# Windowed attention and token mixing on one core: the first batch in a written order, scores and masks by quarters of the array

## Chip, core and metric

One core of one Trainium2 chip runs the whole kernel. The time is the device time of one execution in microseconds, the median of several runs. The engines are TensorE (PE, with its weight loads shown apart as PEld), VectorE (DVE), ScalarE (ACT), GpSimd (POOL) and SyncE (SP); SP and POOL issue the DMAs of this kernel.

## What is computed

Attention with a window of 128 positions and 4 sink positions, over 4 batches, 8 heads, 768 positions, 64 values a head; then an MLP mixer: a token part that works across the 768 positions and a channel part that works across the 512 channels.

```python
scores = scale * np.matmul(q, k.transpose(0, 1, 3, 2))
is_sink = pos[None, :] < int(n_sink)
in_window = (rel >= 0) & (rel < int(window))
scores = np.where(is_sink | in_window, scores, -1000000000.0)
a = np.exp(scores - np.max(scores, axis=-1, keepdims=True))
a = a / (np.sum(a, axis=-1, keepdims=True) + 1e-09)
x = np.matmul(a, v)                       # heads side by side: (4, 768, 512)
xt = x.transpose(0, 2, 1)
h = np.maximum(xt @ w_tok1, 0.0) @ w_tok2
u = x + h.transpose(0, 2, 1)
h2 = np.maximum(u @ w_ch1, 0.0) @ w_ch2
out = u + h2
```

All inputs and the output are fp32; matmuls run in bf16.

## The kernel before

**Tiling.** Two heads make a pair; there are 16 pairs, four in each batch, numbered p = 0 to 15. Rows of a tile of q or k are 128 groups of 6 positions. A pair's q and k are transposed on PE (line 442 for the first pairs, 460 later), by halves of the rows (64 rows, all 128 columns), into PSUM, and evicted to qT and kT (line 118 on DVE, 116 on ACT), the two heads on partitions 0 to 63 and 64 to 127. Scores are made with keys on partitions: for each tile of 128 keys the 256 queries that its window can reach (lines 496 to 503), three pieces g = 0, 1, 2 of two key tiles each. One exp on ACT (line 509) goes over a piece. The values then follow by `pv` (line 555, first batch) or `sink_values` and `values` (lines 597 and 631), with a column of ones that gives the sum of the weights; DVE takes its reciprocal and multiplies into x_sb (lines 576 and 579, 616 and 619).

**Masks.** In the first batch, for all pieces but one, PE writes the mask into PSUM ahead of the scores: a matmul of the identity with a tile of zeros and -32768 (`masked`, lines 471 to 484, over all 128 rows and columns), to which the scores are added. In the later batches, and for that one piece, DVE multiplies by a mask of zeros and ones after the exp (line 516).

**Sinks.** The first four keys of each pair are copied out of the transposed k into a small tile of their own, `kTs` (`sink_columns`, line 410, two copies a pair). `score_sinks` (line 530) makes the scores of two pairs with them, in four matmuls of 64 rows, 32 columns and 512 queries. The sinks' values of the first batch are loaded by SP in four small DMAs in fp32 (line 188) and cast by POOL (line 984).

**Loads.** q and k of the first four pairs come by SP in fp32, 384 KB each (line 81), and are cast by ACT, DVE or POOL (line 979). SP's program has pairs 0 and 1 first, then the four small loads of the sinks' values, then pairs 2 and 3 (lines 131, 188 and 193). All other q, k, v and the weights come on POOL's queue, cast to bf16 on the way (lines 94, 102, 127); v of pair 0 is issued early, at line 194. The order on that queue is v 0 to 3 with the two token weights among them, pair 4, half of the first channel weight (`w_ch1`, in four quarters), pair 5, and so on.

**Order.** A planner (`Plan`, line 238) runs when the program is built. Each unit of PE work has a cost, what it depends on and the PSUM banks that it needs; other work (casts, evictions, exps, loads) has a cost for each engine that could do it. `run` (line 310) goes through planned time and takes the unit that can begin soonest. In the first batch it chooses among six lists (line 808): scores, masks, transposes, values, and token work of the two halves of the channels. After that the units of channel mixing of one batch (`main`) are mixed with attention and token work of the next (`side`). Nothing is decided on the chip: the engines run their lists in order and wait on semaphores. There are two score banks `sc` (each of 2 x 2 KB a partition) and four banks `mx`.

At the start PE runs seven matmuls on a tile of ones (`keep_warm`, line 138) while the first loads are on their way.

Of the kernel before, what the change touches and what calls it, by code (L numbers as in the profile page):

```python
# [9 lines left out]
FP32 = mybir.dt.float32  # L10
# [6 lines left out]
def kernel(  # L17
# [29 lines left out]
    MASKED_BY_PE = [(p, g) for p in range(NHP) for g in range(NT // 2) if (p, g) != (NHP - 1, 0)]  # L47
# [5 lines left out]
    pt_pool = ctx.enter_context(tc.tile_pool(name="pt", bufs=2))  # L53
# [8 lines left out]

    def bank(tag, *shape, dtype=FP32, slot=None):

        n = given[tag].pop(0) if slot is None else slot
        return psum.tile([P, *shape], dtype, name=f"ps_{tag}", tag=f"{tag}{n}", bufs=1)
# [64 lines left out]
    raws = {p: load_raw(p) for p in range(2)}  # L131
    vs = {}


    ones = singles.tile([P, 4 * P], BF16)
    in_order(nc.vector.memset(ones, 1.0))

    def keep_warm(n, slot):
        ps = bank("mx", 4 * P, slot=slot)
        for _ in range(n):  # L140
            mm(ps, ones[:, 0:P], ones, start=True, stop=True)

    keep_warm(7, 0)


# [4 lines left out]
    MASKED = -32768.0  # L150
    mask_add = singles.tile([P, 4, 2, P], BF16)
    mask_adds = [mask_add[:, ts(n, 2)] for n in range(2)]
    in_order(nc.vector.memset(mask_add, 0.0))
# [12 lines left out]
    ))  # L166
    in_order(nc.gpsimd.memset(mask_add[0:n_sink, 2], 0.0))
# [3 lines left out]
    NKB = 2  # L171
    kTb = [singles.tile([P, S], BF16, name=f"kT{n}") for n in range(NKB)]

    kTs0 = singles.tile([P, NHP, 2, D], BF16, name="kTs")
    kTs = [kTs0[:, n] for n in range(NHP)]
# [6 lines left out]
    in_order(nc.vector.memset(kTs0, 0.0))  # L182
    v_sink_f = singles.tile([P, NHP, 2, D1], FP32)
    in_order(nc.vector.memset(v_sink_f, 0.0))
    for n in range(4):
        i, odd = n // 2, n % 2
        rows = slice(D * i + ODD * odd, D * i + ODD * odd + n_sink)
        in_order(nc.sync.dma_start(
            out=v_sink_f[rows, odd::2, i, 0:D],
            in_=v[0].rearrange("(p o i) s d -> i o s p d", i=2, o=2)[i, odd, 0:n_sink],  # L190
        ))
        in_order(nc.vector.memset(v_sink_f[rows, odd::2, i, D:D1], 1.0))
    raws.update({p: load_raw(p) for p in range(2, NHP)})
    vs[0] = load_v(0)
# [19 lines left out]
    SWITCH = 95.0  # L214
    FIRST = 1800.0
# [22 lines left out]
    class Plan:  # L238
# [59 lines left out]

        def commit_pe(self, op, t):
            for tag, banks in op.need.items():  # L300
                given[tag] = [n for _, n in self.slots(tag)[:len(banks)]]
                for n, readers in zip(given[tag], banks):
                    self.held[tag][n] = readers
            op.fn()
            self.free["PE"] = t + op.cost["PE"] + SWITCH * (op.half != self.half)
            self.half = op.half
            op.done = self.free["PE"] + PE_OUT + SEM
            self.pending.extend(op.then)
# [85 lines left out]
    def prepare(p):  # L394

        kT, ks = kTb[p % NKB], kTs[p % NHP]
# [13 lines left out]
        def sink_columns(e):  # L410
            c = ODD * (p % 2)
            first = (tiles["ps_k", p][:, 0] if parts == 1 else tiles["ps_k", p][0])[:, 0, 0:n_sink]
            for i in range(2):
                copy(e, ks[ds(D * i, D), i, c:c + n_sink], first[ds(D * i, D)])

        free = ([("sk", p - 2)] if p >= 2 else [], [("s", p - NKB)] if p >= NKB else [])
# [4 lines left out]
        for n, name in enumerate(("qT", "kT")):  # L421
# [3 lines left out]
            for part, op in enumerate(done[name, p]):  # L425
                op.urgent = (3 - part) * (p < NHP)
        tiles["kT", p] = kT
        done["kTs", p] = Op(
            {"ACT": 440.0, "DVE": 400.0}, sink_columns, [("sk", p - NHP)] if p >= NHP else [],
        )  # L430

    def turn(p, n):
# [3 lines left out]
        def run():  # L436
            ps = [bank("mx", NT, D, dtype=BF16) for _ in range(2)]
            tiles["ps_" + name, p] = [t.rearrange("d j p -> d p j") for t in ps]
            for j in range(NT):
                for x in range(2):  # L440
                    rows = ds(D * x, D)
                    in_order(nc.tensor.transpose(ps[x][:, j], bfs[p, n][rows, j], ident[rows, rows]))  # L442

        readers = [[op] for op in done[name + "T", p]]
        if n:
            readers[0].append(done["kTs", p])
# [5 lines left out]
    def transposed(p):  # L452

        def run():
            ps = bank("sc", 2, 8 * P, dtype=BF16)[:, :, 0:2 * NT * D].rearrange("d x (n j p) -> d x n j p", n=2, j=NT)
            for n in range(2):
                for j in range(NT):
                    for x in range(2):
                        rows = ds(D * x, D)
                        in_order(nc.tensor.transpose(ps[:, x, n, j], bfs[p, n][rows, j], ident[rows, rows]))  # L460
                tiles["ps_" + "qk"[n], p] = ps[:, :, n].rearrange("d x j p -> d x p j")

        then = [*done["qT", p], *done["kT", p], done["kTs", p]]
# [3 lines left out]

    def width(g):
        return 3 * P if g == NT // 2 - 1 else 4 * P

    def masked(p, g):

        def run():
            ps = tiles["ps_s", p, g] = bank("sc", 2, 4 * P)
            for i in range(2):
                mm(
                    ps[:, i, 0:width(g)], ident,
                    mask_adds[g == 0].rearrange("p k n q -> p (k n q)")[:, 0:width(g)], start=True, stop=False,
                )

        x = done["exp", p, g] = Op({}, None)
        deps = [done["tk", 0]] if p == 0 else []
        done["mask", p, g] = unit(width(g) * 0.84, run, deps, {"sc": [[x]]})
        return done["mask", p, g]

    def scores(p, g):


        by_pe = ("mask", p, g) in done

        def run():
            if ("pT", p) not in tiles:
                tiles["pT", p] = pt_pool.tile([P, 2, NT, 2, P], BF16, name="pT")
            if not by_pe:
                tiles["ps_s", p, g] = bank("sc", 2, 4 * P)
            for k in range(2):
                kt = 2 * g + k
                nq = 2 if kt < NT - 1 else 1
                for i in range(2):
                    mm(  # L500
                        tiles["ps_s", p, g][:, i, ds(2 * k * P, nq * P)], tiles["kT", p][ds(D * i, D), ts(kt, P)],
                        tiles["qT", p][ds(D * i, D), kt * P:(kt + nq) * P], start=not by_pe, stop=True,
                    )
# [4 lines left out]
        def exp(e):  # L508
            in_order(nc.scalar.activation(  # L509
                part(tiles["pT", p][:, :, ds(2 * g, 2)]), tiles["ps_s", p, g][:, :, 0:width(g)], AF.Exp, scale=scale,  # L510
# [7 lines left out]
        x = done["exp", p, g] if by_pe else Op({}, None)  # L518
        x.cost, x.fn, x.deps = {"ACT": 190.0 + 1.5 * width(g)}, exp, [done["pv", p - 2]] if p >= 2 else []
        x.urgent = 2 * (p < NHP)  # L520
        then = [x]
        if not by_pe:
            then.append(Op({"DVE": 100.0 + 1.2 * width(g)}, mask, [x, done["masks"]]))
# [3 lines left out]
        deps += [done["mask", p, g]] if by_pe else []  # L527
        return piece(width(g) * 0.47, run, deps, {} if by_pe else {"sc": [[x]]}, then, [("s", p)])

    def score_sinks(p):  # L530


        def run():
            pT_sink = pt_pool.tile([P, (NT - 2) * P], BF16, name="pT_sink")
            tiles["ps_sk", p] = bank("mx", (NT - 2) * P)
            for n in (p - 1, p):
                tiles["pT_sink", n] = pT_sink
                for i in range(2):
# [3 lines left out]
                        tiles["ps_sk", p][ds(D * i + c, ODD)], kTs[n % NHP][rows, i, ds(c, ODD)],  # L542
# [6 lines left out]
        x = Op({"ACT": 580.0}, exp, [done["pv", p - 2]] if p >= 2 else [])  # L549
        for n in (p - 1, p):  # L550
            done["p", n, NT] = x
        deps = [d for m in (p - 1, p) for d in [done["kTs", m], *done["qT", m]]]
        return piece(225, run, deps, {"mx": [[x]]}, [x], [("sk", p - 1), ("sk", p)])

    def pv(p, half):
# [31 lines left out]
        n.urgent = r.urgent = (1 + 1.5 * (p >= NHP // 2)) * (p < NHP)  # L587
# [9 lines left out]
    def sink_values(p):  # L597
# [4 lines left out]
        def run():  # L602
            for i in range(2):
                tiles["ps_o", p, i] = bank("mx", NT, D1)
            for qt in range(2, NT):
                for i in range(2):
                    rows = ds(D * i, D)
                    mm(
                        tiles["ps_o", p, i][:, qt], tiles["pT_sink", p][rows, ts(qt - 2, P)], vsk[rows, i],
                        start=(qt == 2), stop=False,  # L610
                    )
# [120 lines left out]
    def turned_u(b, g, tag="mx"):  # L732
# [4 lines left out]
        def run():  # L737
            if tag == "sc":
                both = bank("sc", 2, 8 * P, dtype=BF16)[:, :, 0:nct * NT * D]
# [334 lines left out]
```

## Time and profile before

| | |
|---|---|
| median of 3 runs | 209.35 us (209.11 to 209.48) |
| the profiled execution: its time | 209.19 us |
| its span in the profile | 207.4 us |
| instructions | 5087 |
| HBM read / written | 26.75 MB / 6.29 MB |
| POOL's DMA queue (q0) | 67232 packets, 11.80 MB |
| SP's DMA queue (q1) | 5968 packets, 9.45 MB |
| exps of the window's scores on ACT (line 509) | 48, 44.3 us |
| first channel matmul (`uT,w_ch`) | starts at 31.2 us |
| first matmul of the second channel weight (`w_ch,v1T`) | starts at 53.0 us |

Busy times of the engines overlap, so they don't add up to the span. Line 109 is the helper through which all matmuls are recorded; they are told apart by the names of the tiles written and read. `64*128` is a matmul that uses 64 rows and 128 columns of the array. Matmuls are pipelined: the duration of one has the way through the array in it, so what a matmul costs in a row of them is read from the distance of the starts. Times in lines of the timeline and of windows are from the start of the span.

### The profile page before, as it was taken

The numbers are of one execution on the slowest core, as the hardware profiler recorded it, in microseconds if no ns is written. First come the engines' busy times: TensorE is split into PE (matmuls) and PEld (weight loads), VectorE is DVE, ScalarE is ACT, GpSimd is POOL, SyncE is SP. The second block draws the span as 40 slices with busy tenths as digits, with TensorE's granted clock in tenths as the row PEclk, the third lists the DMA queues.
The fourth block names the chain that finished last, engine by engine and source line by source line (L and its number), as shares of the span: only waits on it lengthen the run. The fifth ranks groups of instructions, "written<-read, shape, count | busy, mean of one in ns | idle before, by whom it ended". The sixth has DMA issues, their size and how long they took to land.

```text
span 207.4 us, 5087 instructions
## 1 busy us (share of the span) xinstructions
PE 200.7 (97%) x2161; PEld 119.5 (58%) x2161; DVE 114.7 (55%) x246; ACT 113.9 (55%) x208; POOL 67.2 (32%) x86
## 2 busy tenths in 40 slices
PE   6899999999999999999999999999999999999994
PEld 2355885566665565557656645666756445665443
DVE  4686654757768666866586462767583521000222
ACT  4699767868807526868584141869651103773000
POOL 6199678696499991630000000000000000000000
PEclk9999999999999999999999999999999999999999
DMA  6999999999999999695001112100001122000222
GB/s 204 281 240 148 167 187 183 165 166 199 167 174 156 215 174 204 71 82 38 3 0 55 51 54 101 51 5 0 3 0 54 51 101 104 0 0 0 101 104 101
DMA packets 73223, 21.57 MB, mean 104 GB/s; under 512 B 63217, under 2 KB 70257, under 8 KB 73201
## 3 DMA queue, kind: packets, MB, share of 16 engines
q0 software_dynamic: 67232, 11.80, 72.3%
q1 hardware_dynamic: 5968, 9.45, 12.9%
q8 instruction: 17, 0.28, 0.5%
q14 instruction: 6, 0.04, 0.1%
HBM read 26.75 MB, written 6.29 MB: 159 GB/s over the span
## 4 chain that ended last, share of the span: by engine, by line
PE 91%; DVE 4%; DMA 2%; ACT 2%; issue 0%; SPq 0%
PE ps_mx L109 77%; PE ps_sc L109 8%; PE ps_sc L460 2%; DMA k_f<-in_k_dram 2%; PE ps_mx L442 1%; DVE x_sb L619 1%; DVE kT L118 1%; PE ps_mx L749 1%; ACT qT L116 1%; PE ps_mx L112 1%; ACT pT L509 0%; DVE uT L118 0%; ACT v1T L122 0%; DVE recip L616 0%; DVE u_sb L720 0%
## 5 line engine op out<-in xcount | busy, mean ns | idle before, releaser
L109 PE MATMUL ps_mx<-uT,w_ch 128*128 128x384 bf16 x384 | 68.3, 326 | 1.3 <-DVE x_sb L619 0.9
L109 PE MATMUL ps_mx<-w_ch,v1T 128*128 128x512 bf16 (+2 forms) x312 | 65.7, 363 | 0.0
L122 ACT ACTIVATE v1T<-ps_mx 128x384 bf16<-128x384 f32 x74 | 36.2, 492 | 28.7 <-PE ps_mx L109 18.3
L509 ACT ACTIVATE pT<-ps_sc 128x1024 bf16<-128x1024 f32 (+1 forms) x48 | 44.3, 952 | 11.3 <-PE ps_sc L109 10.8
L109 PEld LDWEIGHTS <-w_ch 128*128 128x128 bf16 x384 | 35.3, 98 | 26.1 <-DVE x_sb L619 3.1
L109 PEld LDWEIGHTS <-v1T 128*128 128x128 bf16 x312 | 29.0, 98 | 29.0 <-issue 0.2
L888 DVE TENSOR_TENSOR o_sb<-ps_mx,u_sb 128x512 f32<-128x512 f32 x23 | 15.9, 690 | 39.3 <-PE ps_mx L109 39.0
L94 POOL DMA_DIRECT2D q_bf<-in_q_dram x24 | 19.7, 823 | 5.6 <-DMA w_ch<-in_moe_w_ch_dram 2.2
L109 PEld LDWEIGHTS <-w_tok 128*128 128x128 bf16 x192 | 18.4, 98 | 4.6 <-issue 0.7
L94 POOL DMA_DIRECT2D k_bf<-in_k_dram x24 | 19.6, 820 | 3.7 <-DMA w_ch<-in_moe_w_ch_dram 3.7
L118 DVE COPY kT<-ps_sc 128x768 bf16<-128x768 bf16 x11 | 10.5, 958 | 17.3 <-ACT qT L116 17.3
L102 POOL DMA_DIRECT2D v_aug<-in_v_dram x16 | 16.4, 1028 | 9.4 <-ACT pT L509 6.2
L720 DVE TENSOR_TENSOR u_sb<-ps_mx,x_sb 128x512 bf16<-128x512 f32 x20 | 12.7, 685 | 8.3 <-PE ps_mx L109 8.3
L516 DVE TENSOR_TENSOR pT<-pT,mask_main 128x1024 bf16<-128x1024 bf16 (+1 forms) x24 | 14.5, 619 | 2.5 <-ACT pT L509 2.5
L109 PE MATMUL ps_sc<-qT,kT 64*128 64x256 bf16 x192 | 15.9, 270 | 0.0
L109 PE MATMUL ps_mx<-v_aug,pT 128*128 128x65 bf16 x352 | 15.3, 194 | 0.0
L109 PEld LDWEIGHTS <-pT 128*128 128x128 bf16 x352 | 13.6, 98 | 2.3 <-issue 0.6
L124 DVE TENSOR_SCALAR v1T<-ps_mx 128x384 bf16<-128x384 f32 x22 | 12.1, 554 | 3.8 <-PE ps_mx L109 3.3
L116 ACT ACTIVATE qT<-ps_sc 128x768 bf16<-128x768 bf16 x11 | 8.9, 811 | 7.5 <-PE ps_sc L460 7.3
L109 PE MATMUL ps_mx<-h1T,w_tok 128*128 128x256 bf16 x96 | 12.6, 273 | 0.0
L109 PE MATMUL ps_mx<-x_sb,w_tok 128*128 128x256 bf16 x96 | 12.0, 273 | 0.0
L619 DVE TENSOR_TENSOR x_sb<-ps_mx,recip 128x384 bf16<-128x384 f32 x22 | 11.4, 551 | 0.1
(72 smaller groups left out, 153.7 us busy)
## 6 DMA issues: line engine op xcount, KB each, us to landing
out_dram<-o_sb SPq DMA_DIRECT2D x23, 256.0 KB, 2.0
v_aug<-in_v_dram POOLq DMA_DIRECT2D x16, 192.0 KB, 6.5
w_ch<-in_moe_w_ch_dram POOLq DMA_DIRECT2D x8, 384.0 KB, 8.7
q_bf<-in_q_dram POOLq DMA_DIRECT2D x24, 96.0 KB, 6.7
k_bf<-in_k_dram POOLq DMA_DIRECT2D x24, 96.0 KB, 5.6
q_f<-in_q_dram SPq DMA_DIRECT2D x4, 384.0 KB, 5.9
k_f<-in_k_dram SPq DMA_DIRECT2D x4, 384.0 KB, 6.2
w_tok<-in_moe_w_tok_dram POOLq DMA_DIRECT2D x2, 384.0 KB, 7.4
```

Of the source, the lines that this page charges most:

```text
L94: in_order(nc.gpsimd.dma_start(out=out[:, h], in_=rows[:, h]))
L102: in_order(nc.gpsimd.dma_start(out=v_aug.rearrange("p i t d -> p (i t) d")[:, :, 0:D], in_=v[b].rearrange("h s d -> (h s) d")[2 * hp * S:2 ...
L109: in_order(nc.tensor.matmul(*args, skip_group_check=True, **kwargs))
L116: in_order(nc.scalar.activation(out, in_, AF.Copy))
L118: in_order({"DVE": nc.vector, "POOL": nc.gpsimd}[e].tensor_copy(out=out, in_=in_))
L122: in_order(nc.scalar.activation(out, in_, AF.Relu))
L124: in_order(nc.vector.tensor_scalar_max(out=out, in0=in_, scalar1=0.0))
L509: in_order(nc.scalar.activation(part(tiles["pT", p][:, :, ds(2 * g, 2)]), tiles["ps_s", p, g][:, :, 0:width(g)], AF.Exp, scale=scale,))
L516: in_order(nc.vector.tensor_tensor(out=pt, in0=pt, in1=m, op=ALU.mult))
L619: in_order(nc.vector.tensor_tensor(out=x_sb[b][:, :, ds((2 * hp + i) * D, D)], in0=tiles["ps_o", p, i][:, :, 0:D], in1=tiles["recip", p, i ...
L720: in_order(nc.vector.tensor_tensor(out=u_part(b, g, s0, n), in0=tiles["ps_u", b, g, s0], in1=x_sb[b][:, s0:s0 + n, c0:c0 + cn], op=ALU.add,))
L888: in_order(nc.vector.tensor_tensor(out=o_sb.rearrange("p (g c) -> p g c", g=2), in1=u_rows(b, st), in0=tiles["ps_out", b, st].rearrange("p ...
```

## The change

Seven edits go together.

- **SP's queue** has the eight loads of q and k of the first four pairs back to back. The sinks' values are loaded by POOL in four DMAs straight into the bf16 tile; the fp32 tile and its cast go. v of pairs 0 and 1 are issued by the planner, after the casts of q of pairs 1 and 2, instead of at the head of the program.
- **Quarters.** Transposes, scores and the sinks' values use 64 rows and 64 columns of the array, where they used 64 rows and 128 columns: a transpose or a score matmul becomes two. A quarter of 64 keys is scored against 192 queries (256 for the first), the blocks of the score bank that no quarter writes are filled once by ACT with -32768. Where a transposed tile overwrites such a block, DVE clears it (`cleared`).
- **Masks of the first batch** are added inside the unit of the scores, by quarters (`add_masks`): four matmuls of 64x64 by 256 columns and two by 64. This now holds for all twelve pieces. The 0/1 masks for the later batches are made by DVE after a planned 28 us, not in the first microseconds.
- **Sink scores** read the first 32 columns of kT itself; `kTs` and its copies go. kT has four buffers instead of two, pT three instead of two.
- **The first batch's order** is a written string of unit names, one list instead of six.
- **x in the token part** is added by DVE for all units of the first batch (four of six had it added by PE).
- **Fill.** While the planned time is under 17 us, `fill` puts matmuls of the ones by quarters into the planned gaps of PE; the planner counts PE work double before 13 us.

The diff, cut to its core:

```diff
-    MASKED_BY_PE = [(p, g) for p in range(NHP) for g in range(NT // 2) if (p, g) != (NHP - 1, 0)]
+    FIRST_BATCH = (
+        "q0 k0 q1 s01 s02 k1 s00 x1 s12 q2 s11 k2 s10 q3 s21 o01 k3 s20 o00 o10 s22 o11 x3 s31 s30 o21 h01 "
+        "s32 o20 o30 h00 o31 u00 u04 h10 h11 t00 u02 t04 u10 u12 t02 u14 t10 t12 t14"
+    )
+    NPT = 3
...
+    sc = [psum.tile([P, 2, 2, 4, D], FP32, name=f"ps_sc{n}", tag=f"sc{n}", bufs=1) for n in range(TAGS["sc"])]
...
-    raws = {p: load_raw(p) for p in range(2)}
+    raws = {p: load_raw(p) for p in range(NHP)}
...
+    def keep_warm(n, slot, columns=4 * P, half=False):
+
+        ps = bank("mx", columns, slot=slot)
         for _ in range(n):
-            mm(ps, ones[:, 0:P], ones, start=True, stop=True)
+            for x in range(1 + half):
+                rows = ds(D * x, D) if half else slice(0, P)
+                mm(ps[rows], ones[rows, rows], ones[rows, 0:columns], start=True, stop=True)
...
+    for t in sc:
+        for lo, n in ((D, 0), (0, 3)):
+            in_order(nc.scalar.activation(
+                t[ds(lo, D), :, :, n], ones[ds(lo, D), 0:4 * D].rearrange("p (i k q) -> p i k q", i=2, k=2), AF.Copy,
+                scale=MASKED,
+            ))
...
-    v_sink_f = singles.tile([P, NHP, 2, D1], FP32)
-    in_order(nc.vector.memset(v_sink_f, 0.0))
+    in_order(nc.vector.memset(v_sink0, 0.0))
     for n in range(4):
...
-        in_order(nc.sync.dma_start(
-            out=v_sink_f[rows, odd::2, i, 0:D],
+        in_order(nc.vector.memset(v_sink0[rows, odd::2, i, D:D1], 1.0))
+        in_order(nc.gpsimd.dma_start(
+            out=v_sink0[rows, odd::2, i, 0:D],
             in_=v[0].rearrange("(p o i) s d -> i o s p d", i=2, o=2)[i, odd, 0:n_sink],
         ))
-        in_order(nc.vector.memset(v_sink_f[rows, odd::2, i, D:D1], 1.0))
-    raws.update({p: load_raw(p) for p in range(2, NHP)})
-    vs[0] = load_v(0)
...
+        def fill(self, t):
+
+            n = int((min(t, FILLED) - self.free["PE"] - 100.0) / 214.0)
+            free = self.slots("mx")
+            if n > 0 and free and free[0][0] <= self.free["PE"]:
+                keep_warm(n, free[0][1], 2 * P, self.half)
...
+    def turn_quarters(outs, rows_by_columns):
+
+        for x in range(2):
+            for y in range(2):
+                rows, columns = ds(D * x, D), ds(D * y, D)
+                in_order(nc.tensor.transpose(outs[x][columns], rows_by_columns[rows, columns], ident[rows, rows]))
...
+    def cleared(key, readers):
+
+        op = Op({"DVE": 400.0}, lambda e: in_order(nc.vector.memset(tiles["ps_turned", key][0:D, :, :, 3], 0.0)), readers)
+        op.urgent = 2
+        return op
...
+    def add_masks(ps, g):
+
+
+        for y in range(2):
             for i in range(2):
...
+                rows, keys = ds(D * i, D), ds(D * y, D)
+                m = mask_add[rows, 0:2, :, rows]
+                if g == 0 and y == 0:
+                    mm(ps[keys, i, 0, 0:3:2], ident[rows, rows], mask_sink[rows, 0:2], start=True, stop=False)
+                    mm(ps[keys, i, 1, 0:3:2], ident[rows, rows], m[:, 1], start=False, stop=False)
+                else:
+                    mm(ps[keys, i, :, y:y + 3:2], ident[rows, rows], m, start=True, stop=False)
+        for i in range(2):
+            rows, keys = ds(D * i, D), ds(0, D)
+            m = mask_sink[rows, 2] if g == 0 else mask_add[rows, 0, 1 - i, ds(D * (1 - i), D)]
+            mm(ps[keys, i, 0, 3], ident[rows, rows], m, start=False, stop=False)
...
+            ps = tiles["ps_s", p, g] = bank("sc")
+            if by_pe:
+                add_masks(ps, g)
             for k in range(2):
...
+                for y in range(2):
+                    a = 4 * g + 2 * k + y
+                    nq = min(4 if a == 0 else 3, 2 * NT - a)
+                    for i in range(2):
+                        rows = ds(D * i, D)
+                        mm(
+                            ps[ds(D * y, D), i, k, y:y + nq], tiles["kT", p][rows, ts(a, D)],
+                            tiles["qT", p][rows, D * a:D * (a + nq)], start=not by_pe, stop=True,
+                        )
...
-                        tiles["ps_sk", p][ds(D * i + c, ODD)], kTs[n % NHP][rows, i, ds(c, ODD)],
+                        tiles["ps_sk", p][ds(D * i + c, ODD)], tiles["kT", n][rows, 0:ODD],
...
-            tokens[g] += [mix_u(0, g, st, 2, g == 0 or st == 2) for st in range(0, NT, 2)]
...
+                units[f"u{g}{st}"] = lambda g=g, st=st: mix_u(0, g, st, 2, (g, st) in [])
...
-    plan.free.update(PE=3000.0, ACT=2200.0, DVE=3900.0, POOL=4100.0)
-    plan.queue = 14300.0
-    plan.landings.append(11500.0)
+    plan.free.update(PE=4450.0, ACT=2200.0, DVE=3900.0, POOL=4100.0)
+    plan.queue = 9600.0
...
+    CAST_BY = (('ACT',), ('DVE', 'POOL'), ('POOL',), ('DVE',), ('DVE',), ('DVE',), ('POOL',), ('DVE', 'POOL'))
...
+    for p in range(2):
+        done["v", p].deps.append(("q_bf", p + 1))
```

In the string a letter is the kind of unit and the figures its place: q0 and k0 are the transposes of pair 0, s01 the scores of pair 0, piece 1, x1 the sink scores of pairs 0 and 1, o01 the values of pair 0, second half, and h, u, t the token part of batch 0 by halves of the channels. PE runs them in this order and passes none.

## The prediction

> **What bounds the kernel now.** I read the engine shares and the slices first, then the PE timeline from the start, then the queues that feed it.
>
> ```profile
> PE 200.7 (97%) x2161; PEld 119.5 (58%) x2161; DVE 114.7 (55%) x246; ACT 113.9 (55%) x208; POOL 67.2 (32%) x86
> DMA  6999999999999999695001112100001122000222
> 10.90:31.16 20.26, 20.09 (x309) 13.98 (x305) 14.14 (x36) 16.73 (x27) 17.05 (x21) 1.00 1.74 181
> ```
>
> PE is busy 97% of the span. The last line is one stretch: its ends, its length, then the busy time of PE, weight loads, DVE, ACT and POOL, the granted clock, the DMA share and GB/s. This is the first batch, from about where matmuls reach full speed to the first channel matmul (`uT,w_ch`, 31.16). PE has 0.17 us of idle there. So a microsecond of PE work taken out of it ends it a microsecond sooner, until another limit is met. The DMA slices stand at 9 from 5 to 83 us: that is the nearest other limit.
>
> ```profile
> 1.46 3.17 PE L109 MATMUL ps_mx<-ones 128*128 128x512 bf16 x7 [1.46 <-DVE ones L136]
> 6.03 1.89 PE L109 MATMUL ps_sc<-mask_add,ident 128*128 128x512 bf16 x4
> 11.00 0.60 PE L109 MATMUL ps_sc<-mask_add,ident 128*128 128x512 bf16 x2
> ...
> 34.25 0.35 PE L460 MATMUL ps_sc<-ident,q_bf 64*128 64x64 bf16 x12
> 34.43 0.34 PE L460 MATMUL ps_sc<-ident,k_bf 64*128 64x64 bf16 x12
> ...
> 38.12 0.40 PE L109 MATMUL ps_mx<-qT,kTs 64*32 64x512 bf16 x4
> 38.45 0.50 PE L109 MATMUL ps_mx<-uT,w_ch 128*128 128x384 bf16 x2
> ```
>
> Columns: start, duration, what. A 512-column matmul takes about 430 ns before 10.9 (seven in 3.17 with the tail) and 216 ns after. The 24 transposes of a pair run from 34.25 to 34.61, twelve from 34.25 to 34.43: 29 ns for two. The line at 38.12 is the one that this change hangs on. Four matmuls of 512 columns, two on each half of the rows, at different columns of the array, leave PE 0.33 us later. One stream of 512 is 0.216; what is left, about 0.1, is the change of mode to 128*128. Four small tiles therefore ran in the time of one.
>
> ```profile
> 7.80 0.37 SPq L81 DMA_DIRECT2D q_f<-in_q_dram  x1
> 8.84 0.37 SPq L81 DMA_DIRECT2D k_f<-in_k_dram  x1
> 7.81 0.56 DVE L118 CAST q_bf<-q_f 128x768 bf16<-128x768 f32 x1 [0.77 <-DMA q_f<-in_q_dram]
> 8.85 0.56 DVE L118 CAST k_bf<-k_f 128x768 bf16<-128x768 f32 x1 [0.48 <-DMA k_f<-in_k_dram]
> 20.62 1.53 POOL L127 DMA_DIRECT2D w_ch<-in_moe_w_ch_dram  x2
> DMA to landing us min/median/max: 6.3/8.7/10.4
> ```
>
> SP issues the last q, k loads only at 7.80 and 8.84, each just as the loads of pair 1 land: twelve loads (eight big, four of the sinks' values) were queued and the ninth to twelfth wait for earlier ones. The last line is of `w_ch`: its first quarter, issued at 20.62, lands about 8.7 later, 29.3. The first channel matmul began 1.9 after that.
>
> **The change, part by part.**
>
> *Masks by quarters.* Over the two stretches up to 31.16 the mask matmuls are 22; by the distance of their starts they hold PE 1.8 + 0.7 us before 10.9 and 3.1 after (five pairs of 512 columns and three of 384, at 216 and 163 a matmul), 5.6 in all. In their place come twelve sets: four tiles of 256 columns together (109 ns, the distance of 256-column matmuls: twelve `x_sb,w_tok` from 26.09 to 27.40) and two tiles of 64 (29): 0.14 each, 1.7, and some 0.3 more where they run at half speed. Gain 3.6.
>
> *Mode changes.* Masks and transposes now share a mode with the scores. I count 23 changes of mode in PE's order from 4.8 to 31.15; the written order has about 13 (five groups of 128-wide work, and two in and out of each sink score). Ten at 0.095 (from the 38.12 line): 0.95.
>
> *x added by DVE, not PE:* eight `x_sb,ident` at 109 ns, 0.87. Four u_sb moves go from ACT (0.60) to DVE (0.69): both have room, 14.1 and 16.7 of 20.26.
>
> *Scores by quarters* need 192 columns for most key quarters where 256 were streamed: by sets, 107+107, 107+107, 107+53 ns become 107+80, 80+80, 80+53: 107 ns a pair, 0.43 for four pairs and 1.28 for the other twelve.
>
> So the first batch loses 3.6 + 0.95 + 0.87 + 0.43 = 5.9 us of PE work; by PE alone it would end at 25.3. It won't get all of that, for two reasons.
>
> *Loads.* The eight raw loads go without the four small ones between. k0 landed at 4.96 (its cast starts then), and pair 1's k came 1.04 after its q. Six more at 1.04 to 1.15 end at 11.2 to 11.9, where I read 14.7 for the last (issued 8.84, landing 5.9 later). The first v load, which before ran among them, now waits for a cast of q and comes behind: a v load lands some 1.6 after the one before it (two issued at 10.25, the next use of the queue 2.0 later). So everything behind it on POOL's queue comes about 1.5 earlier, bounds 0 (the DMA engines move the same bytes) and 3.1 (no cost of the v load). The first `w_ch` quarter then lands at 27.8, bounds 26.2 to 29.3. I take the first channel matmul at 28.2: the next matmuls there need this quarter, the only side work ready is the two turns of pair 4 (0.35). Gain of this stage: 3.0.
>
> *POOL and the written order.* POOL now issues the sinks' loads, four, after its mask work (free at 3.6). Price of one: from 0.33 (SP's four took 1.30) to 1.03 (a v load); I take 0.8, near the 0.77 of `w_ch`, being on the same engine: POOL is free at 6.8, bounds 4.9 to 7.7. Behind them stands the cast of q1 (0.84), and PE's list puts turn q1 ahead of the first scores s01. First exp then: 6.8 + 0.84 + 0.3 (twelve transposes at half speed) + 0.6 = 8.6, bounds 7.7 to 9.5; now 8.51. From there ACT has 12 exps (0.92 and 0.70 from start to start) and two sink exps of 0.5: 11.2 us, with some 2 of evictions, to 21.8; then o31 (0.46) and h, u, t of both halves, of which 5.3 of PE work is left: 27.6. This agrees with the limit by loads, which is why I don't take more than 3.0. The ACT writes of masked quarters (4, about 0.4 each) fit in ACT's idle 2.02 to 3.99; fill matmuls take only time planned as gaps.
>
> *Quarter transposes and sinks' values behind 31 us.* Transposes of pairs: 11 pairs x 12 sets, turned u: 6 x 12 (144 instructions of 24), pair 4: 12 sets; sinks' values 11 x 4. That is 260 sets, each of four instead of two. No row shows a four-tile set of 64 columns. Lower end: nothing (the 64*32 sets: four started 3 ns apart inside one stream). Upper end: each half of the columns after the other, twice 29 ns: 7.5 us. Nearest is the 64*32 row, so 3 ns a set: 0.8.
> The Trainium skill, "TensorEngine Tiling (Array Packing)", section Restrictions and Gotchas, says that column tiling excludes Fast Weight Load, and "TensorE: Matmul & The Clock Gate", section LDWEIGHTS, gives columns/1.2 ns for a load. An estimate by these is 53 ns for 64 columns, 24 more than 29, some 6 us in all and no gain left. The 32-column loads of the row at 38.12 agree with no such price, but they are hidden behind 512 columns and half as wide.
>
> *Clearing and evictions.* Eleven pairs lose their sink-column copies (two of about 0.16 each, on ACT or DVE); a DVE clearing of 64x256 in PSUM comes in twelve times, 0.27 to 0.49 (memsets of 256 and 520). It stands on DVE behind the kT copy and before the next norm, whose bank PE awaited five times for 0.4 to 0.5 (one: 0.24 idle at 46.28). Worth 0 to 12 x 0.35 = 4; most are covered by channel matmuls, so 0.2. The third pT buffer and four kT buffers take waits away that PE doesn't show: 0.
>
> Sum: -3.0 - 1.28 + 0.8 + 0.2 = -3.3. The profiled execution took 209.19 (span 207.4, 1.8 around it), 0.16 under the median 209.35. **205.9.**
>
> **Rivals.**
> 1. *Loads don't come earlier.* The DMA engines were full anyway, v_sink's bytes are nothing, so `w_ch` lands at 29.3 and PE waits there: gain 1.6 + 0.3, 207.3. For: DMA at 9 tenths throughout. Against: 2.85 us between k0 and q1 where 1.04 suffices.
> 2. *PE alone decides.* Loads gain 3.1, first exp at 7.7, stage end 26.2 and transposes at no cost: -5.0 - 1.28, 202.9 to 204.5, middle 203.7.
> 3. *Weight loads of quarters bind (slower).* Sets of 64 columns take two loads one after the other, 58 ns instead of 29, on the 260 sets: +7.5; the first batch's turns cost 1.4 more, hidden by the loads' limit. -3.0 - 1.28 + 7.5 = +3.2: 212.4. It decides from (3.0 + 1.28)/260 = 16 ns a set, 45 ns. For: 64-column loads are nowhere in the trace. Against: the four-tile row.
> 4. *The order written out blocks.* q1's cast late on POOL, PE stands before s01, no other unit may pass; with first exp at 9.5 and each of some five casts late by 0.3, the stage ends at 30.5: 208.5.
>
> **Chances.** Forecast 0.45 (204.9 to 206.8), rival 1 0.19, rival 2 0.14, rival 3 0.15, rival 4 0.07. Measurements of this kernel tell 0.2% (0.4 us) from no change. Faster: 0.45 + 0.19 + 0.14 + two thirds of rival 4 and the mild end of 3 = 0.80; same 0.04; slower 0.16. The range 202.8 to 210.0 leaves out most of rival 3 and the fast tail of 2; forecast alone 204.9 to 206.8.
>
> **What would show it.** First `uT,w_ch` matmul at 27.5 to 29 with `w_ch` landing just before it; masks about 2 us of PE; last raw k landed before 12.5; the 48 transposes of a pair in 0.35 to 0.45; first exp near 8.6. Wrong if 48 transposes take 0.6 or more (rival 3), if the first channel matmul starts after 30 (rivals 1 and 4, told apart by whether PE there waits for DMA or idles before 15 us), or if what is gained at 28 is given back by 55, where PE would wait for loads.

## The result and the profile after

The changed kernel takes 211.17 us (median of 4, 211.07 to 213.02), the kernel before 209.23: a ratio of 1.0107 with a 95% interval of 1.0072 to 1.0143. It is slower by about 1%, where 205.9 was forecast. The profiled execution took 211.07, its span 209.1.

Three lines of the windows view of the changed kernel. Columns: ends of the stretch, its length, busy time of PE, weight loads, DVE, ACT and POOL, granted clock, DMA share, GB/s.

```profile
6.60:9.20 2.60, 0.11 (x16) 0.00 (x1) 1.33 (x3) 0.49 (x1) 2.60 (x5) 0.81 1.03 372
9.20:14.50 5.30, 5.23 (x172) 4.16 (x174) 3.23 (x7) 4.36 (x7) 5.30 (x6) 0.50 1.69 224
14.50:33.65 19.15, 16.04 (x376) 13.42 (x366) 13.76 (x33) 11.32 (x18) 15.14 (x19) 0.99 1.80 161
```

PE stands still from 6.6 to 9.2 while POOL is busy all the time. Then it works at a granted clock of 0.50. And from 14.5 to the first channel matmul at 33.65 it has 3.1 us of idle, where this stage had almost none before. The page says the same in its rows of the clock and of instruction DMAs:

```profile
PEclk9759999999999999999999999999999999999999
...
q8 instruction: 23, 0.38, 0.7%
```

The same two rows of the kernel before:

```profile
PEclk9999999999999999999999999999999999999999
...
q8 instruction: 17, 0.28, 0.5%
```

The changed kernel has 23 packets for 3028 matmuls and as many weight loads, where it was 17 for 2161: one packet of 16 KB for some 130 matmuls with their loads.

The first idle, in the timeline (start, duration, engine, line, what; in brackets the idle before and what ended it):

```profile
5.54 2.57 POOL L208 DMA_DIRECT2D v_sink<-in_v_dram  x4 [1.94 <-DVE v_sink L203]
8.11 1.03 POOL L126 CAST q_bf<-q_f 128x768 bf16<-128x768 f32 x1
...
9.20 0.54 PE L455 MATMUL ps_mx<-ident,q_bf 64*64 64x64 bf16 x24 [2.49 <-POOL q_bf L126]
...
9.77 0.49 ACT L124 ACTIVATE qT<-ps_mx 128x384 bf16<-128x384 bf16 x1 [2.52 <-PE ps_mx L455]
10.37 1.72 ACT L546 ACTIVATE pT<-ps_sc 128x1024 bf16<-128x1024 f32 x2
```

The first exp of the kernel before:

```profile
8.51 1.02 ACT L509 ACTIVATE pT<-ps_sc 128x1024 bf16<-128x1024 f32 x1 [1.45 <-PE ps_sc L109]
```

In the changed kernel the first exp starts at 10.37, where it stood at 8.51, and ACT waited 2.52 us for PE ahead of it. q1 itself had landed at 6.77. POOL couldn't cast it, since its four loads of the sinks' values came first, and those waited 1.94 us for a DVE memset of their tile.

The other two long waits of PE:

```profile
17.44 0.33 PE L117 MATMUL ps_mx<-v_aug,pT 128*128 128x65 bf16 x5
19.23 0.19 PE L117 MATMUL ps_mx<-v_aug,pT 128*128 128x65 bf16 x1 [1.46 <-issue]
...
23.98 0.32 PE L117 MATMUL ps_mx<-v_aug,pT 128*128 128x65 bf16 x5
25.80 0.33 PE L117 MATMUL ps_mx<-v_aug,pT 128*128 128x65 bf16 x5 [1.51 <-issue]
```

PE stops in the middle of a unit, between two matmuls of one kind, for 1.5 us, and no engine or load is named: "issue". Counted in weight loads from the start, the stops come after number 351 and number 477. The packets of PE's instruction queue start at 11.54, 16.88 and 23.45 and take 0.9 to 1.0 each, so each stop ends some 1.4 after the end of a packet.

### The profile page after: what moved, and what is told of

The parts are those of the page before. It is cut to its first block, busy times and chain, and to the rows that moved or that the text cites. A ratio compares the mean times of both kernels' runs of the same rounds, so it can differ in the third digit from the quotient of the medians.

```text
span 209.1 us, 6785 instructions
## 1 busy us (share of the span) xinstructions
PE 196.9 (94%) x3028; PEld 122.5 (59%) x3028; DVE 115.9 (55%) x247; ACT 111.1 (53%) x193; POOL 70.8 (34%) x90
## 4 chain that ended last, share of the span: by engine, by line
PE 89%; DVE 4%; POOL 2%; issue 2%; ACT 1%; ACTq 0%
PE ps_mx L117 77%; PE ps_sc L117 6%; PE ps_sc L455 3%; PE ps_mx L455 2%; POOL v_sink L208 1%; DVE u_sb L757 1%; PE ps_mx L120 1%; POOL q_bf L126 0%; ACT pT L546 0%; DVE kT L126 0%; DVE uT L126 0%; ACT qT L124 0%; POOL mask_add L178 0%; ACT uT L124 0%; POOL mask_add L182 0%
## 5 line engine op out<-in xcount | busy, mean ns | idle before, releaser
L130 ACT ACTIVATE v1T<-ps_mx 128x384 bf16<-128x384 f32 x77 | 37.8, 491 | 31.4 <-PE ps_mx L117 21.6
L117 PEld LDWEIGHTS <-w_ch 128*128 128x128 bf16 x384 | 35.6, 98 | 24.1 <-issue 1.4
L757 DVE TENSOR_TENSOR u_sb<-ps_mx,x_sb 128x512 bf16<-128x512 f32 x24 | 15.1, 684 | 6.7 <-PE ps_mx L117 6.7
L117 PE MATMUL ps_mx<-v_aug,pT 128*128 128x65 bf16 x352 | 15.3, 194 | 3.0 <-issue 3.0
L117 PE MATMUL ps_sc<-qT,kT 64*64 64x192 bf16 (+3 forms) x384 | 16.0, 254 | 0.0
L117 PEld LDWEIGHTS <-kT 64*64 64x64 bf16 (+1 forms) x416 | 10.4, 111 | 5.7 <-issue 3.8
L132 DVE TENSOR_SCALAR v1T<-ps_mx 128x384 bf16<-128x384 f32 x19 | 10.3, 544 | 4.6 <-PE ps_mx L117 4.3
L117 PE MATMUL ps_mx<-h1T,w_tok 128*128 128x256 bf16 x96 | 12.1, 272 | 0.0
```

The source lines that it names most:

```text
L117: in_order(nc.tensor.matmul(*args, skip_group_check=True, **kwargs))
L130: in_order(nc.scalar.activation(out, in_, AF.Relu))
L132: in_order(nc.vector.tensor_scalar_max(out=out, in0=in_, scalar1=0.0))
L757: in_order(nc.vector.tensor_tensor(out=u_part(b, g, s0, n), in0=tiles["ps_u", b, g, s0], in1=x_sb[b][:, s0:s0 + n, c0:c0 + cn], op=ALU.add,))
```

## The experiments

The table gathers what the runs' traces and times say. "Loads" are PE's weight loads before the first channel matmul; "to full clock" is where the granted clock is full from there to the end of the matmuls. "Stops" are those that the profile names "issue", of 0.3 us and more. Ratios are to the kernel before on the same chip. Edits are given below.

| kernel | median us | ratio, 95% interval | first exp | to full clock | loads | stops named "issue" | first channel matmul |
|---|---|---|---|---|---|---|---|
| before | 209.1 to 209.3 | 1 | 8.51 | 10.9 | 377 | none | 31.2 |
| changed | 211.17 | 1.0107 (1.0072 to 1.0143) | 10.37 | 15.0 | 592 | 1.5, 1.5 | 33.6 |
| e1 sinks on SP | 210.05 | 1.0050 (1.0015 to 1.0085) | 10.51 | 14.0 | 592 | 0.9, 1.2 | 33.0 |
| e2 q1 by DVE | 212.19 | 1.0143 (1.0104 to 1.0183) | 8.85 | 17.8 | 592 | 1.5, 1.2, 1.2 | 33.8 |
| e3 40 tiny matmuls | 214.48 | no verdict | 10.16 | 24.1 | 632 | 0.7, 2.0, 1.3 | 36.7 |
| e7 halves | 209.37 | 1.0002 (0.9983 to 1.0021) | 10.74 | 15.3 | 484 | none | 32.0 |
| e4 sinks on SP, halves | 208.23 | 0.9945 (0.9914 to 0.9976) | 10.41 | 12.2 | 484 | none | 30.2 |
| e8 pair 0 first | 211.50 | 1.0107 (1.0072 to 1.0142) | 7.74 | 28.7 | 592 | 1.8 | 34.2 |
| e5 e4 and pair 0 first | 208.10 | 0.9922 (0.9878 to 0.9966) | 7.96 | 17.0 | 484 | none | 31.8 |
| e6 e5 and w_ch1 early | 211.52 | 1.0090 (1.0059 to 1.0122) | 7.96 | 16.8 | 484 | none | 31.1 |
| e10 e4, other order | 210.84 | 1.0065 (1.0028 to 1.0102) | 7.65 | 15.8 | 492 | 1.5 | 33.7 |
| e9 e4 and five ones | 207.69 | 0.9937 (0.9909 to 0.9964) | 10.38 | 10.6 | 489 | none | 30.1 |
| e11 e9, few fills | 207.84 | 0.9921 (0.9894 to 0.9949) | 10.39 | 10.8 | 481 | none | 30.6 |
| e12 e11, q1 by DVE | 208.43 | 0.9957 (0.9927 to 0.9988) | 8.7 | 5.4 | 481 | 0.4, 0.6 | 30.0 |

### The late q1 (e1, e2)

e1: the loads of the sinks' values go back to SP, behind the eight raw ones, with a cast by POOL.

```diff
-        in_order(nc.gpsimd.dma_start(
-            out=v_sink0[rows, odd::2, i, 0:D],
+        in_order(nc.sync.dma_start(
+            out=v_sink_f[rows, odd::2, i, 0:D],
...
+    v_sink = Op({"POOL": 650.0}, lambda e: copy(e, v_sink0, v_sink_f), [landed(13000.0)])
```

> The changed kernel with the sinks' values loaded by SP in fp32 behind the eight raw loads and cast by POOL; nothing else. Theory A (POOL's four issues delay the cast of q1, PE waits 2.5 us at 6.6 and its clock falls to half until 15): q1's cast starts at its landing, 6.8, PE waits about 1.1 us, first exp near 8.8 instead of 10.4, the half clock ends earlier, and the time falls by 1.5 or more, to 209.6 or less. Theory B (the two waits of 1.5 us at 17.6 and 24.1, called issue, set the end of the first batch: PE's instructions come too late): the waits stay or grow, the first channel matmul stays after 32.5 and the time falls by less than 1.

e2: q1's cast by DVE, nothing else.

```diff
-    CAST_BY = (('ACT',), ('DVE', 'POOL'), ('POOL',), ('DVE',), ('DVE',), ('DVE',), ('POOL',), ('DVE', 'POOL'))
+    CAST_BY = (('ACT',), ('DVE', 'POOL'), ('DVE',), ('DVE',), ('DVE',), ('DVE',), ('POOL',), ('DVE', 'POOL'))
```

> The changed kernel with the cast of q1 on DVE instead of POOL, the sinks' loads left on POOL. Theory A: as with the sinks on SP, q1 is cast by about 7.4, PE's wait at 6.6 falls from 2.5 to about 0.9, first exp by 8.8, time 209.6 or less. If POOL's four issues cost by what they do to the v loads behind them instead, there is no gain here, and a gain with the sinks on SP.

e1 gained 1.1 us, between the two theories (its interval and that of the changed kernel just overlap), and its profiled execution doesn't show the mechanism: there q1 landed at 8.40 (15 of its 16 parts by 6.64, the last alone 1.8 later), so PE waited 2.5 us all the same. What that execution has is shorter stops, 0.9 and 1.2. So what the 1.1 consists of stays open. e2 does shorten the wait for q1. PE's timeline of e2, the lines with idle before them:

```profile
7.68 0.54 PE L455 MATMUL ps_mx<-ident,q_bf 64*64 64x64 bf16 x24 [0.97 <-DVE q_bf L126]
...
14.13 0.28 PE L455 MATMUL ps_mx<-ident,k_bf 64*64 64x64 bf16 x9 [1.45 <-issue]
...
19.63 0.19 PE L117 MATMUL ps_mx<-v_aug,pT 128*128 128x65 bf16 x1 [1.18 <-issue]
...
25.93 0.24 PE L117 MATMUL ps_mx<-v_aug,pT 128*128 128x65 bf16 x2 [1.23 <-issue]
```

The wait for q1 is down to 0.97 and the first exp comes 1.5 earlier, as theory A says. And the time is no lower at all: a third stop stands at 14.13, and the other two begin later than in the changed kernel. What PE gained at 7 it lost by 14. The clock was at half from 14.4 to 17.8 as well, but PE still came to its next stop, at 19.63, 1.18 us too early, so the clock didn't set that moment. So the late q1 is real, and by itself it isn't what sets the end.

### Where PE's instructions come from (e3, e7)

e3 puts 40 matmuls of two columns, which nobody reads, into the wait behind k0.

```diff
             op.fn()
+            if op is done["tk", 0]:
+                keep_warm(20, self.spare(), 2, True)
```

> The changed kernel with 40 more matmuls of 2 columns (written to a bank that nobody reads) right behind the transposes of k0, where PE waits 2.5 us anyway. Theory B (fetched blocks of instructions, 127 matmuls with their weight loads): the two waits move 40 matmuls forward in PE's list, from the values o01 (matmul 350) and o20 (477) to matmul 310 and 437 as counted before, in other units, and keep about 1.5 us each. The rival, that these units wait for data (v loads, exps): the waits stay at the same matmuls of o01 and o20. The time itself within 0.7 of the changed kernel in both.

(In the changed kernel the stops lie in o00 and o30, not in the two units that I named; the matmul numbers are the ones meant.) PE's timeline of e3:

```profile
14.23 0.38 PE L457 MATMUL ps_mx<-ident,q_bf 64*64 64x64 bf16 x11 [0.71 <-issue]
...
20.27 0.35 PE L457 MATMUL ps_mx<-ident,k_bf 64*64 64x64 bf16 x19 [2.03 <-issue]
...
25.54 0.19 PE L117 MATMUL ps_mx<-v_aug,pT 128*128 128x65 bf16 x1
27.02 0.25 PE L117 MATMUL ps_mx<-v_aug,pT 128*128 128x65 bf16 x3 [1.30 <-issue]
```

The stops stand after weight loads 223, 351 and 478, numbers that now count the 40 added ones; in the changed kernel it was 351 and 477, in e2 223, 351 and 477. In the list of work they have moved forward by 40: the one after 351 from the values of pair 0 into the transposes of k3. No data that PE works on follows such a count; the supply of instructions does, in blocks of 127 or 128 pairs. The four times of e3 lie between 210.61 and 215.94, and the profiled execution took 214.06, so only the places of its stops are read here, not their lengths or its time.

e7 takes instructions away: the transposes of the first batch and of pair 4 go by halves of the rows again.

```diff
             for j in range(NT):
-                turn_quarters([t[:, j] for t in ps], bfs[p, n][:, j].rearrange("p h d -> p (h d)"))
+                for x in range(2):
+                    rows = ds(D * x, D)
+                    in_order(nc.tensor.transpose(ps[x][:, j], bfs[p, n][rows, j], ident[rows, rows]))
```

> The changed kernel with nothing but the transposes of the first batch and of pair 4 by halves of the rows again: 96 matmuls fewer in the first batch, POOL's four sink loads and the written order as they were. If late instructions made the two waits of 1.5 us: they go or move behind 28 us, first exp stays near 10.4, the channel matmuls start at 30.5 to 31.5 and the time is 208.5 to 209.5. If the late q1 alone made the loss: 210.8 or more.

209.37, which is level with the kernel before and 1.8 under the changed one, though all the rest of the change is in it, the late q1 too (first exp 10.74). Between 6 and 32 us PE's timeline shows three waits of half a microsecond and more, and the channel matmul:

```profile
6.33 0.35 PE L467 MATMUL ps_mx<-ident,k_bf 64*128 64x64 bf16 x12 [0.55 <-DVE k_bf L126]
...
9.46 0.50 PE L467 MATMUL ps_mx<-ident,q_bf 64*128 64x64 bf16 x12 [2.78 <-POOL q_bf L126]
...
22.60 0.83 PE L117 MATMUL ps_mx<-x_sb,w_tok 128*128 128x256 bf16 x6 [0.78 <-PE ps_mx L117]
...
31.95 1.46 PE L117 MATMUL ps_mx<-uT,w_ch 128*128 128x384 bf16 x8
```

The two stops of 1.5 are one of 0.78, again at pair 349, which the profile puts down to PE itself; an instruction packet had ended 1.4 us before PE went on, as with the stops named issue. PE's work up to the channel matmuls is no shorter than in the changed kernel (21.9 us against 21.3, without the matmuls of ones), and its idle is 2.1 us shorter: the gain is in the waits, not in the transposes. The start of the channel matmuls, 32.0, missed the expected 30.5 to 31.5.

### Both (e4)

The edits of e1 and e7 together.

> The sinks on SP as in the first of these runs, and besides the transposes of the first batch and of pair 4 by halves of the rows again (12 instead of 24 for each of q and k), 96 matmuls fewer in the first batch. Theory B: one block of instructions less in the first batch, so at least one of the two long waits goes, and the time is 1 to 2 us under the run with the sinks alone. Theory A alone: as that run, within 0.5 (eight changes of mode of 0.1 and more go the other way).

208.23, faster than before by 0.6% (0.9945, 0.9914 to 0.9976). The two gains add up: 1.1 alone, 1.8 alone, 2.9 together, each uncertain by 0.8 to 1.0 by the intervals. PE had no stop over 0.35 us between 9.1 and 30.2, although q1 was late in this execution too:

```profile
9.13 0.50 PE L468 MATMUL ps_mx<-ident,q_bf 64*128 64x64 bf16 x12 [2.49 <-POOL q_bf L126]
...
30.25 0.98 PE L117 MATMUL ps_mx<-uT,w_ch 128*128 128x384 bf16 x5
```

### The written order and the loads of w_ch (e8, e5, e6, e10)

e8 moves the scores of pair 0 ahead of q1 in the changed kernel, e5 in e4; e10 puts q1 between them.

```diff
-        "q0 k0 q1 s01 s02 k1 s00 x1 s12 q2 ...
+        "q0 k0 s01 s02 s00 q1 k1 x1 s12 q2 ...   (e8, e5, e6)
+        "q0 k0 s01 s02 q1 s00 k1 s12 x1 q2 ...   (e10)
```

e6 is e5 with the first two quarters of w_ch1 ahead of pair 4 on POOL's queue.

```diff
-        queue_pair(NHP + n)
         for w in range(NW // 2 * n, NW // 2 * (n + 1)):
             queue(("ch1", w), load_weights(lambda w=w: load_ch1(w)))
+        queue_pair(NHP + n)
```

> The changed kernel with nothing but pair 0's scores moved ahead of q1 in the written order; quarters everywhere. If instructions bound the first batch, the earlier start only brings the block ends nearer to each other: waits at matmuls 223, 350 and 477 of together 3 to 5 us, time within 0.8 of the changed kernel (211.2). If the late q1 made the loss: 209.5 or less.

> Sinks on SP and halves in the first batch's transposes as before, and in the written order the three scores of pair 0 stand ahead of the transposes of q1. If PE's wait for q1 (2.7 us at 6.4) is a matter of the written order: first exp at about 8 instead of 10.4, no wait of PE over 1.2 us there, the channel matmuls start before 29.5 and the time falls by 0.7 or more against the run without this edit (208.2), unless the first w_ch quarter, which lands near 29.8, holds PE: then by 0.5 at most, with PE waiting for that DMA. If the late start is covered by what follows: within 0.3 of 208.2.

> As the run with pair 0 first, and the first two quarters of w_ch1 are loaded ahead of q, k, v of pair 4. If the landing of w_ch bounds the start of the channel matmuls: they land near 25.5 and 27.5, the channel matmuls start at 28 to 29 and the time is 0.5 to 1.5 lower than with pair 0 first alone. If PE's own work bounds it: the same within 0.4, or slower, as pair 4 comes 4 us later.

> Sinks on SP and halves, with the written order q0 k0 s01 s02 q1 s00 k1 s12 x1 at its head. If the 1.8 us that PE waited ahead of x1 with all of pair 0 first was the evictions of pair 1 behind three exps on ACT: that wait falls below 0.7, and the time is 0.5 to 1 under 208.1. If first exps at 8 don't reach the end, because PE's own work and its instructions bound the stage: 207.8 to 208.5.

With quarters (e8) the earlier start is worth nothing: 211.50, as forecast for late instructions. Of the three stops forecast only the last came, 1.78; a wait of 2.12 for x1, shown below, took most of what the early first exp (7.74) had gained. Without them (e5) it is worth nothing either, 208.10 against 208.23, and I had expected 0.7. The first exp came at 7.96, but PE's timelines show new waits ahead of x1. Of e8, and then of e5:

```profile
11.93 1.08 PE L117 MATMUL ps_mx<-qT,kT 64*32 64x512 bf16 x4 [2.12 <-DVE qT L126]
...
24.85 0.33 PE L117 MATMUL ps_mx<-v_aug,pT 128*128 128x65 bf16 x5 [1.78 <-issue]
```

```profile
12.20 0.85 PE L117 MATMUL ps_mx<-qT,kT 64*32 64x512 bf16 x4 [1.73 <-DVE qT L126]
```

x1 needs both pairs; its turn in the list comes before the evictions of pair 1 are through. e10 moved it, and lost 2.6 us against e4, which neither half of its forecast had: the wait for x1 was gone, but a stop of 1.53 named issue is back at 24.13, and others of 1.4 (for q1) and 0.8 stand ahead of it.

```profile
24.13 0.24 PE L117 MATMUL ps_mx<-v_aug,pT 128*128 128x65 bf16 x2 [1.53 <-issue]
```

Eight more fill matmuls had come into the planned gaps. The stop came back with 492 loads and not with 489 (e9), and in the traces the packet came later: in e10 the third block of instructions began at 18.1 and the packet started at 21.73, 3.6 later; in e9 16.1 and 18.25, 2.2 later, and the next block began at 20.7 without a stop. Why the packet took longer to start is not settled.

e6 brought the first quarter of w_ch1 at 24.2 instead of 27.9. The channel matmuls began at 31.1, only 0.7 earlier than in e5, and the time is 3.4 us higher: pair 4 and 5 come later, and from the first matmul of the second channel weight (52.0) to the second batch's channel matmuls (82.6) it takes 30.6 us where e5 takes 27.0. So this landing didn't bind there, and in the changed kernel the quarter had been there for 3.8 us when the channel matmuls began (29.8 and 33.6).

### The clock (e9, e11, e12)

```diff
+            if op is done["tk", 0]:
+                keep_warm(5, self.spare())
```

This is e9, on top of e4; e11 also sets `FILLED` to 5000, which leaves the eight quarter fills out; e12 is e11 with the cast of e2.

> Sinks on SP and halves in the first batch's transposes (208.2), and five more matmuls of the ones, over the whole array and 512 columns, behind the transposes of k0, where PE waits for q1. If PE's idle there brings the half clock (until 12 to 15 us): the granted clock is full from 8.5 or earlier to the end, the matmuls of 9 to 12 us take half the time, the channel matmuls start at 28.8 to 29.7 instead of 30.2 and the time falls by 0.5 to 1.4. If the half clock is covered (PE then waits for casts and exps instead): within 0.4, with new idle of PE between 10 and 15; where q1 lands early, up to 1 slower.

> The fastest so far (207.7: sinks on SP, halves in the first batch's transposes, five whole-array matmuls behind k0) without the eight quarter matmuls of ones that fill planned gaps. They hold PE about 1 us between 10.9 and 30. If PE's own work bounds the stage, as the trace says: the channel matmuls start 0.3 to 0.9 earlier and the time is 206.8 to 207.4. If the fills only lie in gaps: within 0.2 of 207.7. If they keep the clock full: the half clock ends later than 10.6 or comes back, and the time is over 208.

> As the run without quarter fills, and q1 cast by DVE (0.56) in place of POOL (0.84). By PE's order: the transposes of q1 come 0.3 earlier and the time is 0.1 to 0.4 lower. If DVE is late with the kT of pair 0 instead: the same within 0.2 or slower.

The windows view of e4, then of e9:

```profile
4.70:9.00 4.30, 1.36 (x27) 0.68 (x26) 2.32 (x9) 0.98 (x2) 0.75 (x1) 0.98 0.96 318
9.00:12.20 3.20, 3.07 (x70) 2.32 (x70) 2.39 (x5) 2.21 (x3) 3.20 (x4) 0.50 1.14 303
12.20:30.25 18.05, 17.62 (x385) 14.19 (x381) 14.93 (x36) 13.39 (x20) 16.16 (x21) 1.00 1.82 165
```

```profile
4.70:9.00 4.30, 3.92 (x32) 1.47 (x32) 2.80 (x10) 0.98 (x2) 1.43 (x2) 1.00 0.96 309
9.00:10.60 1.60, 1.54 (x41) 1.42 (x40) 1.04 (x3) 0.71 (x2) 1.60 (x2) 1.00 1.06 399
10.60:30.10 19.50, 18.87 (x418) 14.81 (x411) 16.57 (x38) 14.79 (x22) 17.38 (x22) 1.00 1.88 179
```

PE is kept busy from 4.7 to 9 in e9 (3.92 of 4.30 against 1.36), and its clock is full from 10.6 rather than 12.2. (A clock of 1.00 in the first rows is no proof: no clock event had come before 10.6.) The channel matmuls begin 0.1 earlier, a miss; the median is 0.5 lower, which the intervals of e4 and e9 don't tell from nothing. e11 takes 207.84, within 0.2 of e9, as forecast for fills that lie in gaps only; its channel matmuls begin 0.5 later and not earlier. e12 was to be 0.1 to 0.4 lower than e11 and is 0.6 higher, again within the intervals, though its first exp comes 1.7 earlier. In the profiled execution of e12 the clock was full from 5.4 on, and they began at 30.0. So with few instructions the half clock is mostly covered. The medians of e4, e9, e11 and e12 lie within 0.8 us, and their intervals overlap: no version of these is shown to beat another. e4, e5, e9, e11 and e12 are all shown faster than the kernel before; e11 has the lowest ratio, 0.9921 (0.9894 to 0.9949), e9 the lowest median.

## Why the prediction was wrong, step by step

- **"By PE alone it would end at 25.3."** This is the step that failed. The sum counted the time of the quarters and not their number, and it had no idle of PE in it. From the first matmul (1.46) to the first channel matmul, each matmul taken from its start to the next start less the idle between them:

| kernel | work | matmuls of ones | idle | first channel matmul |
|---|---|---|---|---|
| before | 25.5 | 3.2 | 1.0 | 31.2 |
| changed | 21.3 | 4.4 | 6.6 | 33.6 |
| e7 | 21.9 | 4.1 | 4.5 | 32.0 |
| e4 | 20.7 | 4.5 | 3.5 | 30.2 |

  So work did go, 4.3 us where the sum had 5.9, and 5.6 us of idle came: of the 6.6 in the changed kernel 3.0 are the two stops, 2.5 the wait for q1, 0.7 that for k0. The stops come from the number. 592 weight loads and as many matmuls stand before the first channel matmul, where 377 did. PE's instructions come in blocks of about 127 such pairs. In the changed kernel the second block began at 10.1, the third at 14.3, the fourth at 19.2 and the fifth at 25.8; in the kernel before the first three of these fell at 13.0, 19.8 and 29.3. The third and the fourth block took 4.9 us and 6.6, because PE had to wait for the next; there shorter matmuls gained nothing. (It is no fixed pace: in e8, where the next block had come, one took 3.5 us without a stop.) Taking 108 loads out (e7) gave 1.8 us back; moving the count by 40 (e3) moved the stops by 40. With both parts taken back (e4) the channel matmuls begin at 30.2, still 2.0 after the 28.2 of the forecast, and they begin no earlier than 30.0 in e12, where q1 is early too. What holds this stage at 30 is open.
- **"POOL is free at 6.8, bounds 4.9 to 7.7."** It was 8.1. The four issues took 2.57, 0.64 each, under my 0.8; what I left out is that they wait for the memset of their tile, which stood at the end of DVE's preparations (4.74). With a cast of 1.03 instead of 0.84 the first exp came at 10.37 rather than 8.6. Moving the four loads back to SP gave 1.1 (e1), but not by an earlier q1 in the execution that was profiled, and q1 cast early on DVE gave nothing (e2).
- **"Fill matmuls take only time planned as gaps."** The matmuls of ones held PE 1.2 us longer than before; leaving the eight quarter fills out (e11) showed no gain. PE's idle before q1 was longer than planned, and the clock fell to half from 8.2 to 15.0, where it was full from 10.9 before; the sum had the half clock of the kernel before. With few instructions its cost is at most some tenths (e4 against e9).
- **Loads.** The last raw k landed at 12.4, near the 11.2 to 11.9 of the sum. The first quarter of w_ch1 came at 29.8, not 27.8: POOL issued it at 21.0, 0.4 later than before, not 1.5 earlier, since v of pair 0 was issued at 9.1 instead of 3.5. It didn't bind (e6).
- **Masks, mode changes, x by DVE, scores by quarters.** The masks are done as forecast: a set of six has its scores 0.14 later (21.26 to 21.40), and all of them hold PE 2.2 us, where they held it 6.4. PE changes its mode 15 times on the way to the first channel matmul instead of 24. That the change without the two parts that e4 takes back is worth something shows there; no run takes the parts of this item singly.
- **Quarter transposes.** The line of four 64*32 tiles was the right one to read. A pair's transposes in the changed kernel:

```profile
36.76 0.38 PE L455 MATMUL ps_sc<-ident,q_bf 64*64 64x64 bf16 x24
36.97 0.37 PE L455 MATMUL ps_sc<-ident,k_bf 64*64 64x64 bf16 x24
37.16 0.36 PE L117 MATMUL ps_sc<-qT,kT 64*64 64x256 bf16 x8
```

  The sets of four take 35 ns for q (36.76 to 36.97) and 32 for k (36.97 to 37.16), where two halves took 31 and 29 (34.25, 34.43, 34.61): 3 to 4 more a set, and I had put 3. The 53 ns that I worked out as an estimate from the Trainium skill ("TensorE: Matmul & The Clock Gate", section LDWEIGHTS) don't show here. Rival 3 is out: the time of the quarters was not the matter, and that its 212.4 came nearest to the measured time is luck. From the first channel matmul to the end of the last matmul the changed kernel takes 172.2 us (33.6 to 205.8), the one before 173.3 (31.2 to 204.5): a gain of 1.1, where the sum had 0.3.
- **The rivals.** Number 4 had the first half of the mechanism, q1 late on POOL and PE's list standing, at a chance of 0.07, but its price, 208.5, was still a gain. The mechanism that cost most, instructions that come too late, was in none of them. The page before had a row for it, 17 instruction packets, from which 127 matmuls a packet could be worked out, though PE nowhere stopped for one.

Not tried: whether the blocks come late because the DMA engines are full. The traces speak for it. In the kernel before, the packet started about 2 us or more after a block began at 13.0, 19.8 and 29.3, and 0.2 after one at 101.7, when the loads were over. In the changed kernel, counting 127 to a block, it started 2.4 us after the beginning of a block on the mean of 13 blocks before 95 us, and 0.9 on the mean of the ten behind. An experiment would have had to take loads away that the first batch's successors need.

## What to carry to other kernels

Splitting matmuls into smaller tiles that run side by side saves array time and doubles the instructions. Count them: here PE was fed about 127 matmuls with their weight loads at a time, and where the next block came only 4.9 to 6.6 us after the last, while other loads filled the DMA engines, it stopped in the middle of a unit with nothing named but issue. When work is moved to another engine's queue, look at what that work waits for, and at what now stands behind it. And undo a change of seven edits part by part: here two parts undone turned 1% slower than before into 0.6% faster.

## What the hardware showed unasked

- The stops come after 223, 350 or 351, and 477 or 478 weight loads in seven traces, whatever unit these belong to, and each ends 1.2 to 1.8 us after the end of an instruction packet of 16 KB that took 0.9 to 1.5.
- One part of sixteen of a 384 KB load can be late alone: q1 in e1 had 15 parts by 6.64 and the last at 8.40, while in the changed kernel's profiled execution all were in by 6.77.
- The granted clock went between full and half in pieces of 3.4 us: in e2 full at 4.1, half at 7.5, full at 11.0, half at 14.4, full from 17.8. A piece at half could follow a stop: in e8 PE's stop of 1.78 ended at 24.85, and the clock was at half from 25.3 to 28.7.
